# First chunk of a Fourier-mixing and gated-MLP kernel: another order of the weight pieces, and a later place for the combinations of w_out

## The chip, the cores and the metric

The kernel runs on one core of one Trainium2 chip. The metric is the device time of one execution in microseconds (us). The kernel before took 1979.93 us, the median of 8 runs (1978.81 to 1985.56).

## The reference

Two stages in a row. The first takes the real part of a two-dimensional Fourier transform over sequence and model dimension. The second is an MLP with a hard-swish gate.

```python
x: (8, 3008, 256) float32;  w_in: (256, 2048) float64;  w_out: (2048, 256) float64

X = np.fft.fft(np.fft.fft(x, axis=1), axis=2).real.astype(np.float32)
h = X.reshape(24064, 256) @ w_in
g = h * np.clip(h + 3.0, 0.0, 6.0) / 6.0
out = (g @ w_out).astype(np.float32)
```

[...] 

## The kernel before, in words

**Transform.** The eight sequences are taken as four pairs. The sequence transform is done in two stages on TensorE (`stage1`, `stage2`) with a trip through DRAM (`zd`, loaded back by `load_g`) between them. The result of a group of rows is `q`, with `qn` for one extra column. The transform over the model dimension is not done on the data: it is multiplied into w_in (`fold_w_in`, with the matrix `C`), which gives `W1`, and `WN` for the extra column.

**Weights.** w_in and w_out are cut into 16 pieces of 128 x 512 numbers, listed in `PIECES` (L498). Eight are of w_in (two halves `i` of four column blocks `n`), eight of w_out (two halves of four blocks). A piece goes through these steps:

- `load_w` (L506): a DMA issued by GpSimd brings the words into a tile `st`.
- `exponent_a` (L528, ScalarE, two instructions at L532): the exponent bits into a tile `PM`, twice.
- `mantissa` (L547, VectorE, L553 and L554): the mantissa, into `top`.
- `exponent_b` (L534): the two parts of the exponent are subtracted, either on TensorE by two matmuls into a PSUM bank (L542) or on VectorE into an SBUF tile (L538).
- `exponent_c` (L544, ScalarE): makes a power of two of it.
- `join` (L557, VectorE): mantissa times power of two. For w_in it writes a tile `wi` (L562), for w_out two blocks of `G` (L568).

`head(j)` is exponent_a, mantissa and the issue of a later load; `tail(j)` is exponent_c and join; `unit(j)` is exponent_b of piece j, head of piece j+1, tail of piece j.

`fold_w_in(n, h)` multiplies half `h` of column block `n` of w_in with `C`: 8 matmuls into a PSUM tile (L591). Its copy into `W1` (ScalarE, L602) is put off in a list `copies`. While the kernel is starting, a second set of matmuls of one column each (`pw`, L598) makes the `WN` column; later the column is spread by DMAs of SyncE out of `W1` (L607).

**Steps.** A chunk is 256 rows of `q` and its MLP takes 8 steps, `fc` = 0 to 7. A step is `mlp1` (first product into two PSUM tiles `u` and `v`, L337; then VectorE s, u, v, a, a with two ScalarE relus, L342 to L382) and a second product. Step fc needs the columns fc and fc+8 of `W1`, so it needs column blocks of two blocks of w_in: blocks 0 and 2 of w_in serve steps 0 to 3, blocks 1 and 3 serve steps 4 to 7. In the first chunk the second product is `mlp2_first` (L400): four plain block products with the blocks of w_out as they are. From the second chunk on it is `mlp2` (L414): seven products with a Strassen-like scheme. That one needs combinations of the activations (`combine`, GpSimd, three instructions at L396) and of the weights (`mix_w_out`, GpSimd, four instructions at L577 to L580). `mix_w_out(j)` overwrites one of the plain blocks of steps 2j and 2j+1, so it must follow these steps of the first chunk.

**Order.** The order on each engine is the order in which the program text issues the instructions; no scheduler moves them. During the first chunk the main loop (L794 on) issues, in step s: `mlp1` of step s+1, the pending folds, the pieces `DUE[s][0]`, `mlp2_first` of step s, two DMAs that finish the store of `zd`, and the pieces `DUE[s][1]`; then `mix_w_out(0)` to `mix_w_out(2)` in steps 4 to 6. Later steps issue `mlp1` of step s+2, `combine` of step s+1, and `mlp2` of step s; `mix_w_out(3)` stands in step 9. Outside of the start, an exponent on TensorE takes the PSUM tag `d`, which has one bank, and `u`, `v` take a tag `uv`, which has three.

Of the kernel before, what the change touches and what calls it, by code (L numbers as in the profile page):

```python
# [7 lines left out]
F32 = mybir.dt.float32  # L8
# [50 lines left out]
def kernel(  # L59
# [10 lines left out]
    nc = tc.nc  # L70
    P = nc.NUM_PARTITIONS
# [3 lines left out]
    NF = NFC // 2  # L75
# [118 lines left out]
    def bank(shape, name):  # L194
        if starting[0]:
            return ps_a.tile(shape, F32, tag="acc", name=name)
        return ps_d.tile(shape, F32, tag="d", name=name)
# [129 lines left out]
    def mlp1(ch, fc):  # L327
        gr, of, nq = ch.ck // 2, ch.ck % 2 * TB, ch.nq
        q, qn = ch.pr.q[gr], ch.pr.qn[gr]
        u = ps_h.tile([P, 2, TB], F32, tag="uv", name="u")  # L330
        v = ps_h.tile([P, 2, TB], F32, tag="uv", name="v")
        for blk, ps in ((0, u), (1, v)):

            r = slice(0, P - blk)
            for i in range(2):
                f = fc + i * NF
                nc.tensor.matmul(ps[:, i, 0:nq], W1[r, blk, f * P:(f + 1) * P], q[r, blk, of:of + nq],  # L337
                                 start=True, stop=True)
        s = spool.tile([P, 2, TB], F32, tag="s", name="s")
        for i in range(2):  # L340
            f = fc + i * NF
            nc.vector.scalar_tensor_tensor(s[:, i, 0:nq], qn[:, of:of + nq], WN[:, f:f + 1], u[:, i, 0:nq],  # L342
                                           op0=AL.mult, op1=AL.add)


        a = apool.tile([P, 2, 2, TB], F32, tag="a", name="a")
        t = spool.tile([P, 2, 2, TB], F32, tag="t", name="t")
        ch.a[fc] = a
        if ch.last:
            activate_last(a, t, s, u, v, nq)  # L350
            return
        nc.vector.tensor_tensor(u[:], s[:], v[:], op=AL.add)  # L352
        relu(t[:, 0], u[:], 1.0 / 6.0)
        nc.vector.tensor_tensor(v[:], v[:], s[:], op=AL.subtract)  # L354
        relu(t[:, 1], v[:], -1.0 / 6.0)
        gate(a[:, 0], t[:, 0], u[:])
        rev, tk, vk = (m.rearrange("p i (k n) -> p (i k) n", n=N2) for m in (a[:, 1], t[:, 1], v[:]))
        gate(rev[:, :, ::-1], tk, vk)
# [25 lines left out]
    def combine(ch, fc):  # L384
        a = ch.a[fc][:].rearrange("p m f n -> p (m f) n")[:, :, 0:ch.n]
        c = cpool.tile([P, 4, TB], F32, tag="c", name="c")
        cn = c[:, :, 0:ch.n]

        eng = nc.vector if ch.final and fc == NF - 1 else nc.gpsimd
        add(cn[:, 0:2], a[:, 2:3].to_broadcast([P, 2, ch.n]), a[:, 3::-3], eng)  # L390
        add(cn[:, 2], cn[:, 0], a[:, 0], eng)
        add(cn[:, 3], a[:, 1], cn[:, 2], eng)
        ch.c[fc] = cn
# [6 lines left out]
    def mlp2_first(ch, fc):  # L400
        a = ch.a.pop(fc)
        for h in range(2):
            if fc == 0:
                ch.acc[h] = ps_a.tile([P, 2, TB], F32, tag="acc", name="acc")
            for f in range(2):
                nc.tensor.matmul(ch.acc[h][:], G[:, (B11, B12, B21, B22)[2 * f + h], fc, :], a[:, :, f],  # L406
                                 start=(fc == 0 and f == 0), stop=(fc == NF - 1 and f == 1))
        if fc == NF - 1:
            ch.r = epool.tile([P, 2, 2, TB], F32, tag="r", name="r")
            for h in range(2):  # L410
                for m in range(2):
                    nc.scalar.mul(ch.r[:, m, h], ch.acc[h][:, m], (1 - 2 * m) / WS)
# [82 lines left out]

    NWI, NWO = FF // 512, NF // 2
    WB = 512
    PIECES = [("in", 0), ("in", NWI // 2), ("out", 0), ("in", 1), ("in", NWI // 2 + 1)]  # L498
    PIECES = [(k, n, i) for k, n in PIECES + [("out", j) for j in range(1, NWO)] for i in range(2)]
    assert NWI == 4 and NWO == 4  # L500
    raw, difs, exs, fracs, w = {}, {}, {}, {}, {}

# [30 lines left out]

    def exponent_b(j):  # L534
        pm = [PM[j % 2][:, i].bitcast(F16) for i in range(2)]
        if j >= 4 and j % 2:
            exs[j] = wpool.tile([P, WB], F32, tag="ex", bufs=2, name="ex")
            nc.vector.tensor_tensor(exs[j][:], pm[0], pm[1], op=AL.subtract)  # L538
            return
        exs[j] = ps_h.tile([P, WB], F32, tag="uv", name="ex") if starting[0] else bank([P, WB], "ex")  # L540
        for i in range(2):
            nc.tensor.matmul(exs[j][:], E[:, i], pm[i], start=(i == 0), stop=(i == 1))  # L542
# [40 lines left out]
    def fold_w_in(n, h):  # L583

        nb = WB // 2
        cs = slice(n * WB + h * nb, n * WB + (h + 1) * nb)

        ps = bank([P, 2, nb], "wps") if starting[0] else spare[len(copies) % 2]
        for blk in range(2):
            for i in range(2):  # L590
                nc.tensor.matmul(ps[:, blk], C[:, i, blk * P:(blk + 1) * P],  # L591
                                 w["in", n, i][:, h * nb:(h + 1) * nb], start=(i == 0), stop=(i == 1))
        fs = range(cs.start // P, cs.stop // P)

        pw = bank([P, nb // P], "pw") if starting[0] else None
        for f in fs if starting[0] else ():
            for i in range(2):
                nc.tensor.matmul(pw[:, f - fs[0]:f - fs[0] + 1], w["in", n, i][:, (f % (WB // P)) * P:(f % (WB // P) + 1) * P],  # L598
                                 C[:, i, D - 1:D], start=(i == 0), stop=(i == 1))

        def copy():
            nc.scalar.copy(W1[:, :, cs], ps[:])  # L602
            if pw is not None:
                nc.scalar.copy(WN[:, fs[0]:fs[-1] + 1], pw[:])
                return
            for f in fs:
                nc.sync.dma_start(out=WN[:, f:f + 1], in_=W1[P - 1:P, 1, f * P:(f + 1) * P])  # L607

        copies.append(copy)
# [32 lines left out]
        t = T[r, b].rearrange("p g a k n -> p g (a k n)")  # L642
        nc.scalar.copy(t, Z[r].unsqueeze(1).to_broadcast([N2, NG, 2 * TB]))

    folds, copies = [], []

    def head(j):
        exponent_a(j)  # L650
        mantissa(j)
        if j in NEXT:
            load_w(NEXT[j])

    def tail(j):
        exponent_c(j)
        join(j)
        if j % 2 and PIECES[j][0] == "in":
            folds.extend((PIECES[j][1], h) for h in range(2))

    def unit(j):
        exponent_b(j)
        if j + 1 < len(PIECES):
            head(j + 1)
        tail(j)

    def fold_all():
        while folds:
            fold_w_in(*folds.pop(0))
            if len(copies) == 2:  # L670
                copy_all()

    def copy_all():
        while copies:
            copies.pop(0)()

# [19 lines left out]
    load_g(first, 0)  # L698

    seen = wpool.tile([P, 1], F32, tag="seen", name="seen")  # L700
    nc.gpsimd.tensor_copy(seen[:], first.g[0][:, 0, 0:1])
    for j in range(4, 8):
        load_w(j)

# [7 lines left out]
    head(2)  # L712
    tail(1)
    exponent_b(2)
    fold_w_in(*folds.pop(0))
    head(3)
    tail(2)
    exponent_b(3)
# [2 lines left out]
    for i in range(2):  # L721
        stage2(first, 0, i)
    spread(first, 0)
    fold_w_in(*folds.pop(1))
    copy_all()
    starting[0] = False
    spare = [ps_a.tile([P, 2, WB // 2], F32, tag="acc", name="spare") for h in range(2)]
# [52 lines left out]
    def chunk(s):  # L780
        p, ck, fc = steps[s]
        return chunks[p][ck], fc


    DUE = [((), (6,)), ((7,), (8, 9)), ((10, 11), (12,)), ((13,), (14,)), ((15,), ())] + [((), ())] * 3
    head(4)
    mlp1(*chunk(0))
    exponent_b(4)
    head(5)
    tail(4)  # L790
    fold_all()
    unit(5)
    prev = None
    for s, (p, ck, fc) in enumerate(steps):  # L794
        if ck == 0 and fc == 0:
            at = beside(p)
        for f, a in at.get(ck * NF + fc, ()):
            f(*a)
        if s < NF:

            mlp1(*chunk(s + 1))
            fold_all()
            for j in DUE[s][0]:
                unit(j)
            if s == NF - 1:
                combine(*chunk(NF))
            mlp2_first(*chunk(s))
            for dst, src in later[2 * s:2 * s + 2]:
                nc.sync.dma_start(out=dst, in_=src)
            for j in DUE[s][1]:  # L810
                unit(j)
            if 4 <= s < NF - 1:
                mix_w_out(s - 4)
            if s == NF - 1:
                mlp1(*chunk(NF + 1))
        else:
            if s + AHEAD < len(steps):
                mlp1(*chunk(s + AHEAD))
            if s + 1 < len(steps):
                combine(*chunk(s + 1))  # L820
            if s == NF + 1:
                mix_w_out(NWO - 1)
            if prev and fc < 3:
                if fc > 0:
                    store(prev, fc - 1)
                elif not prev.first:
                    finish(prev)
            mlp2(*chunk(s))
        if fc == NF - 1:
            prev = chunks[p][ck]  # L830
# [81 lines left out]
```

## Time and profile before

| | |
|---|---|
| median of 8 runs | 1979.93 us |
| the profiled execution, its own time | 1979.88 us |
| its span, first to last instruction | 1978.0 us |
| TensorE busy in the span | 1943.8 us (98%) |
| VectorE / ScalarE / GpSimd busy | 1442.0 / 687.0 / 1399.8 us |
| TensorE busy, 50 to 100 us from the start | 38.87 of 50 us, granted clock 0.90 |
| TensorE busy, 150 to 175 us from the start | 25.00 of 25 us, granted clock 1.00 |

A busy time is the sum of the instructions of an engine; matmuls are pipelined, and each lasts a little longer than the distance to the next. The granted clock is the share of TensorE's full clock that the chip let it have. Times in the trace are counted from the first instruction. An idle time carries the name of what ended it. The step's first MLP product of the first chunk begins at 49.81 us; the first seven-product step begins at 131.63 us.

### The profile page before, as it was taken

What the parts mean: (1) busy time and instruction counts of PE and PEld (TensorE: products, weight loads), DVE (VectorE), ACT (ScalarE), POOL (GpSimd) and SP (SyncE); (2) the same over time, 40 slices, a digit from 0 to 9 for tenths busy, and PEclk for the clock granted to TensorE, in tenths of its full rate; (3) what the DMA queues carried; (4) which work ended last, traced back from release to release, by engine and by line L of the source; (5) the groups of instructions that cost most, each with busy time, mean ns of one, the idle gap of its engine ahead of it and who ended that gap; (6) DMA issues with size and microseconds to landing.
All of it is one profiled execution on the core that took longest, in us unless ns stands there. A gap on an engine that the chain in (4) does not pass through costs nothing.

```text
span 1978.0 us, 27573 instructions
## 1 busy us (share of the span) xinstructions
PE 1943.8 (98%) x9110; PEld 1670.9 (84%) x9110; DVE 1442.0 (73%) x2780; ACT 687.0 (35%) x1165; POOL 1399.8 (71%) x1592
## 2 busy tenths in 40 slices
PE   9799999999999999999999999999999999999998
PEld 4568888888998888888898888888889888888887
DVE  6786767667787776776777776777678777777776
ACT  5533333333333333333333333333333333333332
POOL 3157778776687787777768877778667667666765
PEclk9899999999999999999999999999999999999999
DMA  8512121121112111220111221212110101111000
GB/s 231 182 39 55 51 56 47 48 56 35 27 36 51 41 49 48 54 60 24 36 32 30 63 55 44 56 41 54 37 22 23 30 14 25 26 23 28 17 21 20
DMA packets 145277, 93.34 MB, mean 47 GB/s; under 512 B 117319, under 2 KB 130635, under 8 KB 145134
## 3 DMA queue, kind: packets, MB, share of 16 engines
q1 hardware_dynamic: 134870, 57.89, 12.2%
q0 software_dynamic: 9472, 33.49, 5.9%
q8 instruction: 72, 1.18, 0.2%
q14 instruction: 71, 0.58, 0.1%
q10 hardware_dynamic: 792, 0.20, 0.0%
HBM read 54.22 MB, written 37.32 MB: 46 GB/s over the span
## 4 chain that ended last, share of the span: by engine, by line
PE 92%; DVE 4%; ACT 2%; DMA 1%; issue 1%; SPq 0%; POOL 0%; DVEq 0%; ACTq 0%; POOLq 0%
PE acc L422 55%; PE v L337 16%; PE u L337 16%; PE ps L213 2%; PE ps L286 2%; DMA xt<-in_x_dram,IX 1%; DVE a L382 1%; DVE s L342 1%; PE acc L406 1%; ACT t L379 1%; ACT PM L532 0%; DVE o L480 0%; PE spare L591 0%; DVE u L352 0%; DVE u L363 0%
## 5 line engine op out<-in xcount | busy, mean ns | idle before, releaser
L396 POOL TENSOR_TENSOR c<-a 128x512 f32<-128x512 f32 (+1 forms) x375 | 468.2, 1248 | 408.1 <-PE acc L422 362.5
L422 PE MATMUL acc<-c,G 128*128 128x256 f32 (+1 forms) x3008 | 696.9, 374 | 0.0
L379 ACT ACTIVATE t<-u,half 128x512 f32<-128x512 f32 (+1 forms) x384 | 260.6, 679 | 1104.9 <-DVE u L352 1025.6
L422 PEld LDWEIGHTS acc<-c,G 128*128 128x128 f32 x3008 | 565.4, 190 | 71.1
L342 DVE SCALAR_TENSOR_TENSOR s<-qn,WN,u 128x256 f32<-128x256 f32 (+1 forms) x768 | 330.3, 471 | 351.9 <-PE u L337 351.4
L422 PE MATMUL acc<-a,G 128*128 128x256 f32 (+1 forms) x2256 | 538.8, 374 | 0.0
L422 PEld LDWEIGHTS acc<-a,G 128*128 128x128 f32 x2256 | 423.4, 190 | 54.9
L337 PE MATMUL v<-q,W 127*128 127x256 f32 (+1 forms) x1536 | 389.1, 375 | 4.2 <-DVE a L382 4.2
L337 PE MATMUL u<-q,W 128*128 128x256 f32 (+1 forms) x1536 | 387.9, 375 | 0.0
L382 DVE SCALAR_TENSOR_TENSOR a<-t,u 128x512 f32<-128x512 f32 (+2 forms) x448 | 263.8, 601 | 102.4 <-ACT t L379 97.3
L337 PEld LDWEIGHTS u<-q,W 128*128 128x128 f32 x1536 | 285.9, 190 | 57.6 <-issue 16.6
L337 PEld LDWEIGHTS v<-q,W 127*128 127x128 f32 x1536 | 288.0, 189 | 44.7 <-DVE a L382 4.6
L396 POOL TENSOR_TENSOR c<-a,c 128x256 f32<-128x256 f32 (+1 forms) x375 | 268.5, 716 | 29.4
L396 POOL TENSOR_TENSOR c<-c,a 128x256 f32<-128x256 f32 (+1 forms) x375 | 268.2, 715 | 29.4
L352 DVE TENSOR_TENSOR u<-s,v 128x512 f32<-128x512 f32 x352 | 245.0, 696 | 38.1 <-DVE s L342 1.8
L382 DVE SCALAR_TENSOR_TENSOR a<-t,v 128x512 f32<-128x512 f32 (+1 forms) x480 | 263.4, 565 | 0.5
L379 ACT ACTIVATE t<-v,half 128x512 f32<-128x512 f32 (+1 forms) x384 | 260.5, 678 | 1.0 <-PE acc L422 0.8
L354 DVE TENSOR_TENSOR v<-v,s 128x512 f32<-128x512 f32 x352 | 243.8, 693 | 0.0
L396 POOL TENSOR_TENSOR r<-w,e 128x256 f32<-128x256 f32 (+1 forms) x92 | 88.7, 986 | 3.6
L430 ACT ACTIVATE e<-acc 128x512 f32<-128x512 f32 (+2 forms) x186 | 84.4, 544 | 3.4 <-PE acc L422 3.3
L480 DVE STREAM_TRANSPOSE o<-r 128x256 f32<-128x256 f32 (+1 forms) x192 | 72.5, 415 | 0.3
L213 PE MATMUL ps<-y,F 94*96 94x512 f32 x120 | 61.3, 601 | 5.2 <-ACT q L289 5.2
(96 smaller groups left out, 798.3 us busy)
## 6 DMA issues: line engine op xcount, KB each, us to landing
out_dram<-o SPq DMA_DIRECT2D x746, 32.0 KB
zd<-z SPq DMA_DIRECT2D x24, 384.0 KB
g<-zd SPq DMA_DIRECT2D x36, 256.0 KB
xt<-in_x_dram POOLq DMA_DIRECT2D x21, 384.0 KB, 4.3
qn<-qd SPq DMA_DIRECT2D x19, 256.0 KB
st<-in_moe_w_in_dram POOLq DMA_DIRECT2D x8, 512.0 KB, 8.3
st<-in_moe_w_out_dram POOLq DMA_DIRECT2D x8, 512.0 KB, 4.0
g<-zd SPq DMA_DIRECT2D x12, 257.0 KB
```

The source lines that it names most:

```text
L213: nc.tensor.matmul(ps[0:PZ], F[0:PR, 0:PZ], y[:, 2 * i:2 * i + 2, :], start=True, stop=True)
L286: nc.tensor.matmul(ps[:, blk, u * P:n].rearrange("p (b k) -> p b k", b=2), g[:, kk, blk * (P + 1):blk * (P + 1) + P], T[:, :, gr, blk, kk, ...
L337: nc.tensor.matmul(ps[:, i, 0:nq], W1[r, blk, f * P:(f + 1) * P], q[r, blk, of:of + nq], start=True, stop=True)
L342: nc.vector.scalar_tensor_tensor(s[:, i, 0:nq], qn[:, of:of + nq], WN[:, f:f + 1], u[:, i, 0:nq], op0=AL.mult, op1=AL.add)
L352: nc.vector.tensor_tensor(u[:], s[:], v[:], op=AL.add)
L354: nc.vector.tensor_tensor(v[:], v[:], s[:], op=AL.subtract)
L379: nc.scalar.activation(t, h, AF.Relu, bias=half[:], scale=scale)
L382: nc.vector.scalar_tensor_tensor(dst, t, 1.0, h, op0=AL.min, op1=AL.mult)
L396: (eng or nc.gpsimd).tensor_tensor(out, in0, in1, op=AL.add)
L422: nc.tensor.matmul(ch.acc[i // 2][:, i % 2, 0:ch.n], G[:, i, fc, :], mv, start=(fc == 0 and i % 2 == 0), stop=(fc == NF - 1), skip_group_c ...
L430: nc.scalar.mul(ch.e[:, k:i + 1, 0:ch.n], ch.acc[i // 2][:, 0:i + 1 - k, 0:ch.n], 1.0 / WS)
L480: nc.vector.transpose(o[:, 0:n // DH, h], ch.r[:, m, h, 0:n].rearrange("p (j i) -> p j i", i=DH))
```

## The change

1. In `PIECES` the second block of w_out moves ahead of the second half of w_in. Before: in 0, in 2, out 0, in 1, in 3, out 1, out 2, out 3. After: in 0, in 2, out 0, out 1, in 1, in 3, out 2, out 3 (two pieces each).
2. `exponent_b`: only the pieces 5 and 15 are subtracted on VectorE; before, 5, 7, 9, 11, 13 and 15. The others go through TensorE and the one bank `d`.
3. The folds are called by name (`fold_now`). Those of blocks 1 and 3 stand in step 3, which has an order of its own (`fourth_step`): `mlp2_first` of step 3 first, then pieces 10 to 13 and the first-half folds between them, then `mlp1` of step 4, then the second-half folds. Every fold with h = 0 makes its `WN` columns by `pw` matmuls, in a `uv` tile; only those with h = 1 use DMAs.
4. In all other steps of the first chunk the second product comes directly after `mlp1`, and the pieces after it. `DUE` follows.
5. `mix_w_out(0)` and `(1)` are issued in step 5, after a one-column copy on GpSimd (`see`) that reads the activations of step 6; `(2)` and `(3)` in steps 8 and 9.

```diff
-    PIECES = [("in", 0), ("in", NWI // 2), ("out", 0), ("in", 1), ("in", NWI // 2 + 1)]
-    PIECES = [(k, n, i) for k, n in PIECES + [("out", j) for j in range(1, NWO)] for i in range(2)]
+    PIECES = [("in", 0), ("in", NWI // 2), ("out", 0), ("out", 1), ("in", 1), ("in", NWI // 2 + 1)]
+    PIECES = [(k, n, i) for k, n in PIECES + [("out", j) for j in range(2, NWO)] for i in range(2)]
...
-        if j >= 4 and j % 2:
+        if j in (5, len(PIECES) - 1):
...
-        pw = bank([P, nb // P], "pw") if starting[0] else None
-        for f in fs if starting[0] else ():
+        pw = ps_h.tile([P, nb // P], F32, tag="uv", name="pw") if h == 0 else None
+        for f in fs if h == 0 else ():
...
-    DUE = [((), (6,)), ((7,), (8, 9)), ((10, 11), (12,)), ((13,), (14,)), ((15,), ())] + [((), ())] * 3
+    DUE = [(6,), (7,), (8, 9), (), (14,), (15,), (), ()]
     head(4)
     mlp1(*chunk(0))
     exponent_b(4)
     head(5)
     tail(4)
-    fold_all()
+    fold_now(0, 1)
+    fold_now(NWI // 2, 1)
+    copy_all()
     unit(5)
+    def fourth_step():
+        mlp2_first(*chunk(3))
+        fold_now(1, 0)
+        unit(10)
+        copy_all()
+        unit(11)
+        exponent_b(12)
+        fold_now(NWI // 2 + 1, 0)
+        head(13)
+        tail(12)
+        copy_all()
+        exponent_b(13)
+        tail(13)
+        mlp1(*chunk(4))
+        fold_now(1, 1)
+        fold_now(NWI // 2 + 1, 1)
+        head(14)
+        copy_all()
...
-            mlp1(*chunk(s + 1))
-            fold_all()
-            for j in DUE[s][0]:
-                unit(j)
-            if s == NF - 1:
-                combine(*chunk(NF))
-            mlp2_first(*chunk(s))
+            if s == 3:
+                fourth_step()
+            else:
+                mlp1(*chunk(s + 1))
+                if s == NF - 1:
+                    combine(*chunk(NF))
+                mlp2_first(*chunk(s))
             for dst, src in later[2 * s:2 * s + 2]:
                 nc.sync.dma_start(out=dst, in_=src)
-            for j in DUE[s][1]:
+            for j in DUE[s]:
                 unit(j)
-            if 4 <= s < NF - 1:
-                mix_w_out(s - 4)
+            if s == 5:
+                see(chunk(s + 1)[0].a[s + 1][:, 0, 0, 0:1])
+                mix_w_out(0)
+                mix_w_out(1)
...
-            if s == NF + 1:
-                mix_w_out(NWO - 1)
+            if s < NF + 2:
+                mix_w_out(s - NF + 2)
```

`see(x)` is `nc.gpsimd.tensor_copy(seen[:], x)`; `fold_now(n, *hs)` calls `fold_w_in(n, h)` for each h; `fold_all`, which took the folds from a list and copied after every two, is gone.

More of the change, by code (lines that the diff above doesn't have):

```diff
@@ L643 @@
         nc.scalar.copy(t, Z[r].unsqueeze(1).to_broadcast([N2, NG, 2 * TB]))
-    folds, copies = [], []
+    copies = []
     def head(j):
@@ L657, in tail @@
         join(j)
-        if j % 2 and PIECES[j][0] == "in":
-            folds.extend((PIECES[j][1], h) for h in range(2))
     def unit(j):
@@ L665, in unit, with fold_now @@
         tail(j)
[L667 to L671, printed above, removed]
+    def fold_now(n, *hs):
+        for h in hs:
+            fold_w_in(n, h)
     def copy_all():
@@ L675, in copy_all, with see @@
             copies.pop(0)()
+    def see(x):
+        nc.gpsimd.tensor_copy(seen[:], x)
     for c in ORDER[0:3]:
@@ L700 @@
     seen = wpool.tile([P, 1], F32, tag="seen", name="seen")
-    nc.gpsimd.tensor_copy(seen[:], first.g[0][:, 0, 0:1])
+    see(first.g[0][:, 0, 0:1])
     for j in range(4, 8):
@@ L714 @@
     exponent_b(2)
-    fold_w_in(*folds.pop(0))
+    fold_now(0, 0)
     head(3)
@@ L723 @@
     spread(first, 0)
-    fold_w_in(*folds.pop(1))
+    fold_now(NWI // 2, 0)
     copy_all()
```

## The prediction

> **What bounds the kernel now.** I read the page, then TensorE's waits, then the first 140 us by windows and by instruction.
>
> ```profile
> PE 1943.8 (98%) x9110; PEld 1670.9 (84%) x9110; DVE 1442.0 (73%) x2780; ACT 687.0 (35%) x1165; POOL 1399.8 (71%) x1592
> PE spare L591 <- ACT W L602: 5.3, 1, 5.3
> PE ps L213 <- ACT q L289: 5.2, 8, 0.7
> PE acc L406 <- DVE G L568: 4.6, 3, 2.5
> PE v L337 <- DVE a L382: 4.2, 7, 1.5
> ```
>
> TensorE bounds the run. Of its named waits, 24.8 us in all, 14.8 lie between 50 and 131.6 us, the first and third of these lines among them; later steps have nearly none (TensorE 25.00 of 25 us between 150 and 175). So the change is worth what it does there, and everything after should move along unchanged. TensorE in the middle of that:
>
> ```profile
> 73.78 1.03 PE L591 MATMUL spare<-wi,C 128*128 128x256 f32 x4
> 80.10 6.18 PE L591 MATMUL spare<-wi,C 128*128 128x256 f32 x16 [5.29 <-ACT W L602]
> 86.12 0.59 PE L542 MATMUL ex<-PM,E 128*128 128x512 f16 x2
> 89.18 1.13 PE L406 MATMUL acc<-a,G 128*128 128x512 f32 x2 [2.47 <-DVE G L568]
> 91.51 1.69 PE L406 MATMUL acc<-a,G 128*128 128x512 f32 x2 [1.21 <-DVE G L568]
> ```
>
> The second pair of folds waits 5.29 us for ScalarE to copy the first pair, and that copy stands behind the relus of step 3, which wait for VectorE. Then pieces 10 and 11 of w_out are awaited, 2.47 and 1.21. The folds that follow take 6.02 us to the next start; the same 16 matmuls took 3.45 at 52.06. The windows say why (columns: TensorE, weight loads, DVE, ACT, POOL, granted clock):
>
> ```profile
> 74.88:78.29 3.41, 0.00 (x0) 0.00 (x0) 3.31 (x6) 0.07 (x1) 2.15 (x3) 1.00 0.35 119
> 78.29:81.70 3.41, 1.60 (x4) 1.34 (x5) 2.88 (x5) 2.24 (x4) 0.00 (x0) 0.50 0.02 0
> 81.70:85.11 3.41, 3.41 (x10) 2.70 (x9) 0.00 (x0) 0.58 (x1) 0.00 (x0) 0.50 0.06 1
> 85.11:88.53 3.42, 1.60 (x8) 0.89 (x6) 0.00 (x0) 2.21 (x4) 0.00 (x0) 1.00 0.06 1
> 88.53:91.94 3.41, 1.56 (x3) 0.59 (x4) 3.20 (x8) 3.33 (x6) 0.07 (x1) 1.00 0.75 214
> 91.94:95.36 3.42, 3.42 (x5) 1.35 (x4) 1.28 (x2) 0.08 (x1) 0.77 (x1) 0.50 0.86 273
> ```
>
> The clock halves at 78.29, returns at 85.11, halves at 91.94, returns at 95.36: all on a grid of 3.41 us. A window busy for 1.56 us or less is followed by half clock; 1.60 was enough to hold it. Loss: 6.02 - 3.44 = 2.6 and, for six records at 91.51, 4.38 - 2.58 = 1.8; together 4.4 us. Last, GpSimd slows VectorE:
>
> ```profile
> 73.07 1.28 DVE L553 TENSOR_SCALAR top<-st 128x512 int32<-128x512 int32 x1
> 74.13 0.80 POOL L578 TENSOR_TENSOR G<-G 128x256 f32<-128x256 f32 x1
> 80.21 0.42 DVE L553 TENSOR_SCALAR top<-st 128x512 int32<-128x512 int32 x1
> ```
>
> The same mantissa instruction takes 1.28 us beside `mix_w_out` and 0.42 alone. From 73.07 to 76.53 VectorE does what takes 1.66 without it: 1.8 us late, in front of the relus and copies just named.
>
> **The change, part by part.** Durations, as start to next start in the timeline: on TensorE first product 1.73, second product 3.44, one fold 1.73, `pw` 0.79, one exponent 0.43. On VectorE a mantissa 1.06, a join 0.60 (w_in) or 0.67 (w_out), the five instructions of a step 3.68 (59.36 to 63.04). On ScalarE a pair of L532 1.33, one L545 0.58. Hand-overs: exponent on TensorE to L545 0.63 (95.89 to 96.52), from there to the join 0.61.
>
> *Added on TensorE.* Four more exponents (pieces 7, 9, 11, 13): 4 x 0.43 = 1.7. Two `pw`: 1.6. Both lie in TensorE's order, none is hidden: +3.3. In return VectorE loses four L538 (0.60 each) and SyncE four small DMAs; neither is on the path there.
>
> *The new order, walked.* Up to 64.00 (second product of step 1) nothing differs but piece 6, a w_out piece whose join is 0.07 longer. Then:
> - Second product of step 1 to 67.44, exponent 7, first product of step 3 to 69.60. Step 2's activations are ready at 68.6, join 7 writes its first block by 70.2, and that is needed at 70.46: the second product of step 2 ends at 73.04 without a wait. Exponent 8 ends at 73.47.
> - Exponent 9 needs the one bank back, so join 8. ScalarE reaches L545 of piece 8 after the relus of step 3 and piece 9's L532, at 74.75; join 8 ends at 76.05. TensorE waits 2.6.
> - Exponent 9, second product of step 3 (to 79.96), fold and `pw` (82.48), exponent 10 (82.91). The pieces 10 to 12 now form a chain through the bank: 0.63 + 0.61 + 0.69 + 0.04 = 2.0 from one exponent to the next, of which TensorE works 0.43. It waits 1.5 for join 10. The second link is 2.5, since the fold's copies and a pair of L532 hold L545 until 85.6: 2.1 for join 11. Exponent 12 ends at 87.39.
> - Fold and `pw` to 89.91, exponent 13, first product of step 4 to 92.07, two folds to 95.53, first product of step 5 to 97.26. Step 4's activations (VectorE from 91.82) are ready at 95.5, so the second product of step 4 ends at 100.70 without a wait.
> - Steps 5 to 7 have no wait on this walk: exponent 14, first and second products to 111.47, `stage2` 0.89, 114.09, 117.53. VectorE is about 2 us ahead each time.
> - First products of steps 9 and 10; the second one's `v` waits 1.55 for the activations of step 9, as now at 130.66 (1.53). The first seven-product step starts at 122.6.
>
> It starts at 131.63 now: 9.0 us gained before any clock loss. Cross-check: waits counted as above, drain included, sum to 7.8 now planned; in the trace they are 13.9 named from 64.00 on, and nine drains of 0.17 (a first product's half lasts 1.03, its start distance is 0.86), 15.5 in all. So -7.7 of waits, -4.4 of half clock, +3.3 of work = -8.8.
>
> *New half-clock windows.* The 2.6 wait, and the 1.5 + 2.1 pair with 0.43 between, can each leave a grid window under 1.6 busy. Where the grid falls against them I can't know. Bounds: none, 0; two full windows, 2 x 1.7 = 3.4. The nearest row is the second drop, also after two gaps of one to three us: 1.8. I take 1.8. [...]
>
> *The mixes moved.* (0) and (1) start when step 6's activations exist, about 105.8, and last 8 x 0.81 = 6.5, to 112.3; they are needed at 122.6. Beside them VectorE has only piece 15's subtraction and join to be slowed, by up to 0.9 (1.10 to 0.69 for L554 at 103.12); the join is due at 108.9 and would end its first block at 108.7: 0. The instructions of a step are not slowed (0.69 beside L578 at 113.96). (2) is new in step 8: 3.1 us, by (3) now (137.81 to 140.92). Queued behind it are combines 10 to 12 and a fold of x. Their first results stand at 136.3, 142.2 and 147.3 now, and TensorE asks at 142.4, 148.1 and 152.8; GpSimd is idle 0.8 ahead of combine 10, so they come 2.3 later, and 3.2 or more stays. Cost 0; bounds 0 and 3.1.
>
> *SyncE.* The four column DMAs of steps 6 and 7 go at 96.6, after the copies; behind them in the queue two `zd` stores, two T loads, and the load of group 1, issued 3.75 after the stores as now (92.40 to 96.15): 104. It took 6 us to clear (96.15 to 102.1), so 110, and `stage2` asks at 111.5. Now it has 18 us to spare, then 1.5. I count 0; up to 2 if it is late.
>
> **Sum.** -9.0 + 1.8 = -7.2. The profiled execution took 1979.88 with 1978.0 in the span; the 1.9 around it stays. 1979.9 - 7.2 = **1972.7**. It stands 0.05 from the median, which I neglect.
>
> **The rivals.**
> - *The bank chain is slower than walked.* For: exponent 10 now stands 86.12 to 89.45, 3.3 from start to end of join, because an L532 pair got ahead in ScalarE's queue; after the change ScalarE has such a pair between all of them. Against: on the walk these pairs fit into the wait. At most four links (9 to 12) at 3.3 in place of 2.0: +5.2, 1977.9. No measurable change.
> - *Half clock holds through step 3.* Place: 76.5 to 97.3, TensorE work there 3.44 + 4 x 1.73 + 2 x 0.79 + 4 x 0.43 + 2 x 1.73 = 17.1; at half clock 17.1 more, less 3.6 of waits that it fills: +13.5 on the walk, 1979.9 - 9.0 + 13.5 = 1984.4, slower. It decides from 9.0 lost, over five windows. For: gaps recur over 14 us. Against: slowed work fills the windows, and one full window brought the clock back (85.11).
> - *GpSimd becomes the bound* in steps 9 to 12: 3.1 of mixing unabsorbed, 1975.8. Against: it stood idle 1.21 at 148.89, 1.18 and 1.87 after.
>
> **How the numbers follow.** A measurement of this kernel tells about 0.2%, 4.0 us, from no change: faster is below 1976.0, slower above 1983.9. Forecast as walked, with 0 to 2 half-clock windows, 0.73, its own range 1970 to 1975.5; GpSimd 0.08, mostly still faster; bank chain 0.13; half clock 0.06. Faster 0.78, no change 0.15, slower 0.07. The range takes the walk's best case and reaches to the bank chain: 1969.0 to 1978.5.
>
> **What would show it.** Right: no wait of `spare` for W; waits of exponents 9, 11, 12 for joins, 2.6, 1.5 and 2.1; the first seven-product step at 122 to 125; mantissas all at 0.42 between 70 and 100; at most two half-clock windows between 73 and 95. Wrong: TensorE waiting for L396 after 122, `stage2` waiting for `g`, links of 3 us, or a first seven-product step past 128.

## The result, and the profile after

The changed kernel took 1976.22 us, the median of 13 runs (1973.19 to 1980.6). The kernel before, run beside it, took 1980.52 us over 35 runs. The ratio is 0.9979, 95% interval 0.9972 to 0.9986: 4.2 us faster, 0.21%, just past the 0.2% that the prediction set as the least that can be told from no change; the interval does not contain 1. The forecast was 1972.7; its range held the time, its gain of 7.2 us was too large. The profiled execution took 1974.02 us with a span of 1972.2.

The page's line of engine totals, and TensorE's waits over the whole run (waiter, what ended it, total, times, longest):

```profile
PE 1944.4 (99%) x9134; PEld 1672.9 (85%) x9134; DVE 1437.7 (73%) x2776; ACT 686.6 (35%) x1167; POOL 1398.7 (71%) x1593
PE ex L542 <- DVE wi L562: 5.6, 3, 2.4
PE ps L213 <- ACT q L289: 5.2, 8, 0.7
PE v L337 <- DVE a L382: 2.3, 5, 1.5
...
PE acc L406 <- DVE G L568: 0.9, 1, 0.9
```

The wait of the folds for ScalarE (5.3 before) is gone, and of the 4.6 us for w_out blocks 0.9 is left. In their place stands one new line, the largest of all: exponents that wait for the join of the piece before, which reads the one PSUM bank that they need, three times, 5.6 us. TensorE there, in order of time:

```profile
73.05 0.59 PE L542 MATMUL ex<-PM,E 128*128 128x512 f16 x2
76.08 0.59 PE L542 MATMUL ex<-PM,E 128*128 128x512 f16 x2 [2.44 <-DVE wi L562]
76.51 3.60 PE L406 MATMUL acc<-a,G 128*128 128x512 f32 x8
79.94 1.89 PE L591 MATMUL spare<-wi,C 128*128 128x256 f32 x8
81.67 0.95 PE L599 MATMUL pw<-C,wi 128*128 128x1 f32 x8
82.48 0.59 PE L542 MATMUL ex<-PM,E 128*128 128x512 f16 x2
84.46 0.59 PE L542 MATMUL ex<-PM,E 128*128 128x512 f16 x2 [1.39 <-DVE wi L562]
86.87 1.01 PE L542 MATMUL ex<-PM,E 128*128 128x512 f16 x2 [1.81 <-DVE wi L562]
87.68 3.62 PE L591 MATMUL spare<-wi,C 128*128 128x256 f32 x8
92.66 1.02 PE L337 MATMUL u<-q,W 128*128 128x256 f32 x4
```

Up to 84.46 the walk holds to a few hundredths (76.09, 82.48 and 84.45 were forecast). Then the same eight fold matmuls that took 1.89 at 79.94 take 3.62 at 87.68, and the first product of step 4 starts at 92.66 instead of 90.34. The windows on the 3.41 us grid (TensorE, weight loads, DVE, ACT, POOL, granted clock):

```profile
81.53:84.94 3.41, 2.02 (x14) 1.31 (x13) 1.18 (x3) 1.83 (x5) 0.00 (x0) 1.00 0.00 0
84.94:88.35 3.41, 1.59 (x5) 1.02 (x4) 2.25 (x4) 2.90 (x5) 0.00 (x0) 0.50 0.00 0
88.35:91.77 3.42, 3.42 (x11) 2.76 (x11) 0.75 (x2) 0.59 (x2) 0.00 (x0) 0.50 0.00 0
```

A window with a granted clock of 0.50 is called a half-clock window from here on. There are two, one after the other: the first was busy for 1.59 us and another followed it; after the second, which was full, the clock was back.

**Where the time went.** The start of a run drifts by a few us between profiled executions (the first product began between 48.98 and 52.61; in the three that began after 51.5 a half-clock window lies near 30 us), and everything after the first seven-product step takes 1846.4 to 1846.9 in every kernel here. So the profiles are best compared by the first chunk, from the first product to the first seven-product step. It is that of one profiled execution; the median is that of 5 to 13 runs (35 of the kernel before), and each ratio is to runs of the kernel before taken beside it, with medians of 1980.16 to 1980.98:

| kernel | first chunk, us | half-clock windows in it | median of its runs, us | ratio to before, 95% |
|---|---|---|---|---|
| before | 81.82 | 3 | 1980.52 | 1 |
| after | 75.61 | 2 | 1976.22 | 0.9979 (0.9972 to 0.9986) |
| after, run again (`c_after`) | 76.90 | 3 | 1975.68 | 0.9978 (0.9969 to 0.9987) |
| `hold3`: after, waits filled | 73.25 | 0 | 1971.89 | 0.9959 (0.9945 to 0.9973) |
| `odd_dve`: after without part 2 | 72.11 | 1 | 1971.48 | 0.9953 (0.9939 to 0.9967) |
| `mix_early`: after without part 5 | 75.00 | 2 | 1977.57 | 0.9984 (0.9975 to 0.9993) |
| `col_dma`: after without `pw` | 74.34 | 2 | 1973.91 | 0.9968 (0.9956 to 0.9980) |
| `before_hold`: before, waits filled | 77.73 | 0 | 1976.11 | 0.9978 (0.9969 to 0.9987) |
| `before_latemix`: before with part 5 | 77.88 | 2 | 1977.19 | 0.9981 (0.9972 to 0.9990) |
| `odd_hold` | 70.71 | 0 | 1970.26 | 0.9948 (0.9935 to 0.9962) |
| `best1` | 69.45 | 0 | 1969.56 | 0.9948 (0.9934 to 0.9962) |
| `best2` | 69.10 | 0 | 1967.48 | 0.9935 (0.9921 to 0.9949) |

### The profile page after: what moved, and what is told of

Its sections match the earlier page's. It is cut to its first block, busy times and chain, and to the rows that moved or that the text cites. A ratio compares the mean times of both kernels' runs of the same rounds, so it can differ in the third digit from the quotient of the medians.

```text
span 1972.2 us, 27615 instructions
## 1 busy us (share of the span) xinstructions
PE 1944.4 (99%) x9134; PEld 1672.9 (85%) x9134; DVE 1437.7 (73%) x2776; ACT 686.6 (35%) x1167; POOL 1398.7 (71%) x1593
## 4 chain that ended last, share of the span: by engine, by line
PE 93%; DVE 3%; ACT 1%; DMA 1%; issue 1%; SPq 0%; DVEq 0%; POOL 0%; ACTq 0%; POOLq 0%
PE acc L422 55%; PE v L337 16%; PE u L337 16%; PE ps L213 2%; PE ps L286 2%; DMA xt<-in_x_dram,IX 1%; DVE a L382 1%; PE acc L406 1%; DVE s L342 1%; ACT t L379 1%; PE spare L591 0%; DVE o L480 0%; DVE u L363 0%; ACT PM L532 0%; DMA T<-in_c_stage_dram 0%
```

## The experiments

**The changed kernel again.** No edit.

> The changed kernel again, for another fall of the 3.41 us clock grid and a tighter ratio. Theory (the walk is right, and the half-clock windows after the waits for the one exponent bank are what was mis-sized): ratio to before 0.998, single runs spread over 1973 to 1981 as the grid falls, and the profile has one to three half-clock windows between 73 and 95 us, with the first seven-product step at 122.6 plus about 1.2 us for each. Rival (the loss against the walk lies elsewhere, in the slowed join of piece 15 or later than 125 us): the same ratio, but a start of the first seven-product step that doesn't go with the number of half-clock windows.

Median 1975.68 over 11 runs (1973.32 to 1980.75). Its profile caught another fall of the grid:

```profile
72.22:75.63 3.41, 1.31 (x5) 0.34 (x4) 3.19 (x6) 3.41 (x6) 0.00 (x0) 1.00 0.60 192
75.63:79.04 3.41, 3.06 (x5) 1.45 (x5) 2.69 (x6) 2.81 (x5) 0.71 (x1) 0.50 0.51 151
...
85.87:89.28 3.41, 2.02 (x5) 0.89 (x5) 2.69 (x5) 2.94 (x5) 0.00 (x0) 0.50 0.00 0
89.28:92.70 3.42, 3.42 (x11) 2.66 (x9) 0.75 (x2) 0.58 (x1) 0.00 (x0) 0.50 0.00 0
```

Here the wait ahead of exponent 9 fell well into a window too. Three windows at half clock, and the first seven-product step at 126.62: four us past the walk's 122.6, where two windows gave 125.44. The start goes with the number of windows, at about 1.2 us each: none, two and three give first chunks of 73.25 (`hold3`, next), 75.61 and 76.90.

**Waits filled with idle matmuls.** The five matmuls of a constant add nothing to the output.

```diff
+    def hold(n):
+        for i in range(n):
+            nc.tensor.matmul(spare[1][:].rearrange("p a b -> p (a b)"), ones[:], C[:].rearrange("p a b -> p (a b)"), start=True, stop=True)
...
             for j in DUE[s]:
+                if j == 9:
+                    hold(2)
                 unit(j)
...
         copy_all()
+        hold(1)
         unit(11)
+        hold(2)
         exponent_b(12)
```

> Adds five idle-time matmuls of the constant C into an unused PSUM tile: two ahead of exponent 9, one ahead of exponent 11, two ahead of exponent 12; 0.86 us each, inside waits of 2.44, 1.39 and 1.81 us. Their results are not used. Theory: no half-clock window is left between 73 and 95 us, so the first seven-product step starts at 122.6 to 123.2 instead of 125.4, the runs spread less, and the ratio to before is 0.995 to 0.997 (1971 to 1974 us). Rival (half clock there is covered by the chain of exponent, ScalarE and join, and costs nothing): 0.998 as without them, or above.

Median 1971.89, ratio 0.9959, five runs within 2.1 us of each other. TensorE in `hold3`:

```profile
82.74 0.59 PE L542 MATMUL ex<-PM,E 128*128 128x512 f16 x2
83.17 1.02 PE L800 MATMUL spare<-C,ones 128*128 128x512 f32 x2
84.72 0.59 PE L542 MATMUL ex<-PM,E 128*128 128x512 f16 x2 [0.53 <-DVE wi L562]
85.15 1.88 PE L800 MATMUL spare<-C,ones 128*128 128x512 f32 x4
87.10 0.59 PE L542 MATMUL ex<-PM,E 128*128 128x512 f16 x2
87.53 1.89 PE L591 MATMUL spare<-wi,C 128*128 128x256 f32 x8
```

The exponents stand where they stood (this execution began 0.2 us later), the work between them is useless, and the fold behind takes 1.89 instead of 3.62. No window is at half clock. The first chunk is 73.25 us; the walk, which had no clock loss, gave 122.6 - 49.8 = 72.8. So 2.4 us of the profiled execution (75.61) and 3.7 of the second one (76.90) were half clock, and by the medians about 4. The granted clock of the single runs agrees: 0.995 to 0.997 in those of the changed kernel, the slowest of them (1980.6) at 0.995 and the fastest (1973.19) at 0.997, and 0.998 to 0.999 in the five of `hold3`.

**Odd pieces back on VectorE.**

```diff
-        if j in (5, len(PIECES) - 1):
+        if j >= 4 and j % 2:
```

> Undoes part 2 of the change alone: pieces 5, 7, 9, 11, 13 and 15 subtract their exponents on VectorE, as before. Theory (the single exponent bank sets the pace of step 3): the wait ahead of exponent 9 is gone, exponents 9 and 11 no longer stand between TensorE and its products, the first product of step 4 starts about 2 us earlier at full clock, and the time falls by 1 to 3 us against the changed kernel (ratio to before 0.9965 to 0.9975). Rival (VectorE is what sets step 3, so that four more instructions of 0.6 us on it cost): 1 to 3 us slower than the changed kernel, 0.9985 to 0.9995.

Median 1971.48, 4.2 us below the 1975.68 of the changed kernel and better than expected. TensorE's waits in `odd_dve`:

```profile
PE ex L542 <- ACT PM L532: 3.1, 5, 1.9
...
PE acc L406 <- DVE G L568: 1.5, 2, 0.9
PE acc L406 <- DVE a L382: 0.7, 1, 0.7
```

No exponent waits for a join any more; the longest wait left is exponent 12, 1.9 us for ScalarE. With every window at full clock (`odd_hold`, below) the first chunk is 70.71 against 73.25: part 2 of the change, which puts these exponents through the one bank, costs 2.5 us; the rest of the 4.2 goes with half-clock windows, one here against two and three. VectorE had most of the room, as it sat idle 4.65 us ahead of join 10 in the changed kernel. Not all: TensorE now waits for it twice where it did not, 0.57 us for the join of piece 7 and 0.75 for the activations of step 3, and the 2.5 are what is left after that.

**Combinations at their old place in the new order.**

```diff
-            if s == 5:
-                see(chunk(s + 1)[0].a[s + 1][:, 0, 0, 0:1])
-                mix_w_out(0)
-                mix_w_out(1)
+            if 4 <= s < NF - 1:
+                mix_w_out(s - 4)
...
-            if s < NF + 2:
-                mix_w_out(s - NF + 2)
+            if s == NF + 1:
+                mix_w_out(NWO - 1)
```

> Undoes part 5 alone: combinations of w_out 0, 1 and 2 issued in steps 4, 5 and 6 and 3 in step 9, without the one-column copy ahead of them. Theory (in the new order of pieces VectorE waits in step 3 anyway, so slowing it there costs nothing): GpSimd runs combination 0 at about 77 us beside a mantissa and a join, combination 1 at about 80 to 83 us in VectorE's idle time, 2 at about 109 us beside piece 15; the ratio stays at 0.998, within 0.5 us. Rival (the later place of the combinations is what the change gained): 2 to 3 us lost, ratio 0.999 to 1.000.

Ratio 0.9984 (0.9975 to 0.9993) against 0.9978 (0.9969 to 0.9987) for the unchanged one: 1.9 us by the medians, with intervals that overlap, and a first chunk of 75.00 us with as many half-clock windows as the 75.61 of the change. The medians speak for the late place and the two first chunks, 0.6 us apart, against it; this run does not settle what it is worth in the new order.

**Combinations late, alone, on the kernel before.** The same edit the other way round on the old order.

```diff
-            if 4 <= s < NF - 1:
-                mix_w_out(s - 4)
+            if s == 5:
+                nc.gpsimd.tensor_copy(seen[:], chunk(s + 1)[0].a[s + 1][:, 0, 0, 0:1])
+                mix_w_out(0)
+                mix_w_out(1)
...
-            if s == NF + 1:
-                mix_w_out(NWO - 1)
+            if s < NF + 2:
+                mix_w_out(s - NF + 2)
```

> Part 5 of the change alone, on the kernel before: combinations 0 and 1 in step 5 after the one-column copy, 2 and 3 in steps 8 and 9, pieces and folds as they were. Theory (in the old order VectorE stood in front of the copies of the folds, so slowing it counted): the mantissas near 73 us take 0.42 us, the wait of 5.29 us falls to about 3.5, 2 to 3 us gained, ratio 0.9985 to 0.999. Rival (the part matters as little in the old order as in the new): 0.9995 to 1.0005.

Ratio 0.9981 (0.9972 to 0.9990), more than expected: this part alone gains 3.8 us by the medians (2.0 to 5.5 by the interval), where the whole change gains 4.2. In this kernel:

```profile
75.45 0.42 DVE L553 TENSOR_SCALAR top<-st 128x512 int32<-128x512 int32 x1
80.70 5.41 PE L591 MATMUL spare<-wi,C 128*128 128x256 f32 x16 [3.50 <-ACT W L602]
```

The mantissa that took 1.28 us beside a combination takes 0.42, and the wait of the folds falls from 5.29 to 3.50, the 1.8 us that the walk had for it. One half-clock window fewer and the wait for step 5's activations, 1.49 us at 110.11 in the kernel before and gone here, make the rest of the 3.9 us by which the first chunk is shorter. By the medians the parts of the change do not add: parts 1 to 4 without part 5 (`mix_early`) gain 3.0, part 5 alone 3.8, both together 4.2. That the late combinations shorten a wait which the new order does not have at all would account for it; the intervals are too wide to show it.

**The half clock of the kernel before.** Seven idle matmuls of a constant, five between the two pairs of folds, two ahead of the second product of step 2.

```diff
             if len(copies) == 2:
                 copy_all()
+                if folds:
+                    keep_awake(5, by=C[:].rearrange("p a b -> p (a b)"))
...
+            if s == 2:
+                keep_awake(2, by=C[:].rearrange("p a b -> p (a b)"))
             mlp2_first(*chunk(s))
```

> The kernel before with seven idle-time matmuls of C (results unused): five between the two pairs of folds where TensorE waits 5.29 us, two ahead of the second product of step 2. It measures the term of 4.4 us for half clock in the kernel before. Theory: no half-clock window between 74 and 100 us, first seven-product step 3 to 4.5 us earlier than 131.6, ratio 0.9975 to 0.9985. Rival (ScalarE and VectorE set the pace there and the slow matmuls were covered): 0.9995 to 1.0005.

Ratio 0.9978, 1976.11 us: filling the waits of the old order gains as much as the whole change. The first chunk is 77.73 against 81.82, so half clock cost the kernel before 4.1 us (4.4 were read off its profile).

**Columns by DMA instead of `pw` in step 3.**

```diff
-        pw = ps_h.tile([P, nb // P], F32, tag="uv", name="pw") if h == 0 else None
-        for f in fs if h == 0 else ():
+        pw = ps_h.tile([P, nb // P], F32, tag="uv", name="pw") if starting[0] else None
+        for f in fs if starting[0] else ():
```

> The changed kernel without the one-column matmuls in step 3: all four later folds spread their columns by DMAs, as before. It measures the term of 1.6 us of added TensorE work. Theory (the matmuls lie on the path and the DMAs would have landed in time): 0.8 to 2 us gained against the changed kernel, ratio 0.9968 to 0.9975; and since these matmuls count as busy in the profile but a window with them still fell to half clock, the number of half-clock windows does not rise without them. Rival (step 4 then waits for its columns): 1 to 3 us lost, VectorE idle ahead of s of step 4, ratio 0.9985 to 0.9995.

Median 1973.91, ratio 0.9968 against 0.9978; first chunk 74.34 against 75.61, both with two half-clock windows. The added matmuls cost 1.3 us of the 1.6 that were counted (1.3 again between `odd_hold` and `best1`, below, where no clock is lost). VectorE does not wait for the columns in step 4: s of that step starts at 93.54, with no idle time ahead of it.

**What was found, put together.** `odd_hold` is `odd_dve` with `hold(2)` ahead of exponent 12. `best1` adds the edit of `col_dma`. `best2` also lets the copy on GpSimd read piece 15's last block:

```diff
-                see(chunk(s + 1)[0].a[s + 1][:, 0, 0, 0:1])
+                see(G[:, B22, NF - 1, 0:1])
```

> The changed kernel with odd pieces subtracted on VectorE and two idle-time matmuls of the constant C (results unused) ahead of exponent 12, where that version waits 1.89 us. Theory (two separate losses: the bank chain, about 2 us, and the half-clock windows, about 2 to 4 us): no half-clock window is left, the first seven-product step starts near 121.5 us when the start of the first product is as in the changed kernel, ratio to before 0.994 to 0.9955. Rival (both versions remove the same loss, the half clock): no gain over either alone, 0.9955 to 0.996.

> Three findings together on the changed kernel: odd pieces subtracted on VectorE, two idle-time matmuls of C ahead of exponent 12 (results unused), and the columns of the later folds by DMA instead of one-column matmuls. Theory (the three losses add up: bank chain, half clock, added matmuls): from the start of the first product to the first seven-product step 69.1 us, against 70.7 without the DMAs and 75.6 to 76.9 in the changed kernel; no half-clock window; ratio to before 0.9935 to 0.9945. Rival (with the rest gone, step 4 waits for its columns): 70.7 us or more, 0.9948 or above.

> best1 with the one-column copy that holds back combinations 0 and 1 reading the last block that piece 15 writes, instead of the activations of step 6. Theory (the join of piece 15, slowed beside combination 0, keeps TensorE 0.36 us in step 6): that join takes 0.75 instead of 1.84 us, 0.3 to 0.4 us gained on the first chunk, within the noise of the time; the combinations end about 4 us later, just before the first combine. Rival (the later combinations hold back the first combines): TensorE waits for GpSimd after the first seven-product step, 0.5 us or more lost.

All three lost every half-clock window in the first chunk: 70.71, 69.45 and 69.10 us. For `odd_hold` 0.9948 is inside what was expected, so bank chain and half clock are two losses. For `best1` the first chunk came out near the 69.1 of the theory, but its time only matched `odd_hold`: 1.3 us of chunk are inside the spread of five runs (1966.62 to 1971.58). `best2` has the lowest ratio, 0.9935 (0.9921 to 0.9949), 12.7 us faster than before by the medians; its own edit is worth 0.35 us in the profile. The join of piece 15 in the changed kernel, and then in `best2`:

```profile
108.61 1.11 DVE L538 TENSOR_TENSOR ex<-PM 128x512 f32<-128x512 f16 x1
109.25 1.06 POOL L578 TENSOR_TENSOR G<-G 128x256 f32<-128x256 f32 x1
110.42 1.84 DVE L568 TENSOR_TENSOR G<-top,ex 128x256 f32<-128x256 f32 x2 [0.69 <-ACT ex L545]
```

```profile
105.24 0.68 DVE L538 TENSOR_TENSOR ex<-PM 128x512 f32<-128x512 f16 x1
106.62 0.76 DVE L568 TENSOR_TENSOR G<-top,ex 128x256 f32<-128x256 f32 x2 [0.70 <-ACT ex L545]
107.52 0.18 POOL L676 COPY seen<-G 128x1 f32<-128x1 f32 x1 [27.67 <-DVE G L568]
```

## Why the prediction was right and where it was off

- *Where the kernel was bound, and that only the first chunk would move*: right. From the first seven-product step to the end it is 1846.37 us before and 1846.76 after.
- *The walk through the new order*: right. Its waits of 2.6, 1.5 and 2.1 (drain included) stand in the profile as 2.44, 1.39 and 1.81 without drain, at its times, and at full clock (`hold3`) the first chunk is 73.25 against its 72.8. With the clock loss taken out of both kernels (`before_hold` and `hold3`) the change is worth 77.73 - 73.25 = 4.5 us; the prediction had 7.7 of waits less 3.3 of work, 4.4.
- *Added work on TensorE, +3.3*: right in place. The `pw` half of it measured 1.3 for 1.6. What the four exponents cost is more than their 1.7 us of work, since they also wait for the bank: 2.5 us in all, but these waits were in the walk.
- *The mixes, cost 0*: off by 0.36 us. Piece 15's subtraction was slowed as reckoned, the join more (1.84 for 0.75), so TensorE's second product of step 6 took 3.96 instead of 3.60. GpSimd did not become the bound, and SyncE's load of group 1 was in time.
- *New half-clock windows, +1.8*: the step that failed, by size. The mechanism was named, with the two gaps that caused it, and its bounds were "none, 0; two full windows, 2 x 1.7 = 3.4". The profiles have two and three windows, 2.4 and 3.7 us, and by the medians (1975.7 to 1976.2 against 1971.89) it is about 4 in a typical run: more windows than were counted, past the upper bound, though each costs less than 1.7. The row I took, the second drop of the kernel before, was a single window followed at once by full work. The first drop in the same table would have told more. It lasts two windows, from 78.29 to 85.11, and lost 2.6: the first of them was busy for 1.60 us at half clock, and half clock followed. So "1.60 was enough to hold it" was read from a window at full clock alone. In the new order work comes in pieces of 0.43 us between waits, the first window at half clock still contained a wait and was busy for 1.59 us (84.94 to 88.35), and half clock followed there too.
- *The sum*: -9.0 + 0.4 + 4.0 = -4.6, against 4.2 to 4.3 measured. The gain at full clock is right; the change has traded 4.1 us of half clock for about as much of its own. That the time lies in the range says little of this term, since the range is 9.5 us wide; and 1976.22 is 0.2 us above the 1976.0 below which the prediction called it faster, a bound set from 1979.9, where the kernel before took 1980.52 beside the change.
- *The rivals*: the bank chain did not run slower than walked. Half clock did not last through step 3. Parts 1, 3 and 4 of the change, the new order itself, were not run apart from each other.

## What to carry to other kernels

When an order is written by hand, walk it at full clock, and then ask of each new wait whether it can cost clock as well: here short pieces of work between waits were followed by 2.4 to 3.7 us of half clock, on top of 5.6 us of waits. A wait that cannot be removed can be filled with idle matmuls; here five of them gained 3.8 us, about as much as the whole reordering had. Parts of a change that remove the same wait are tried one by one, since one alone may give nearly all of it (here, by the medians, the later combinations) while another takes some back (here the exponents on the one bank).

## What the runs showed of the hardware that was not expected

The prediction read off the kernel before that a window busy for 1.56 us falls to half clock and one busy for 1.60 does not. That was no threshold. In both profiles of the changed kernel a window with 2.02 us busy was followed by half clock (81.53 to 84.94 above, and 82.46 to 85.87 in the second), while in `mix_early` this one was not:

```profile
75.48:78.89 3.41, 1.47 (x5) 0.84 (x5) 3.32 (x6) 3.36 (x7) 1.51 (x3) 1.00 0.19 34
78.89:82.31 3.42, 3.42 (x11) 1.88 (x11) 2.46 (x4) 1.08 (x2) 3.26 (x4) 1.00 0.37 137
```

Both windows of the changed kernel contain `pw`, eight records of matmuls with one column each, that the profile shows as 0.95 us busy. `col_dma` has no `pw` in step 3: its window from 82.35 to 85.76 is shown busy for 1.43 us, and it fell too.

So the busy time does not sort the windows. At full clock, windows busy for 0 and 1.56 us (before, 74.88 and 88.53), 1.25 (`odd_dve`, 82.56), 1.31 and 2.02 (`c_after`, 72.22 and 82.46), 1.43 (`col_dma`), 2.02 (after, 81.53) and 2.10 (`mix_early`, 82.31) were followed by half clock; those busy for 1.47 (`mix_early`, above) and 1.60 (before, 85.11) kept the clock. Of the windows at half clock between the first product and the first seven-product step, the five that were followed by another were busy for 1.59 (after, 84.94) to 2.29 us (`col_dma`, from 85.76 on), and those busy for 2.97 (`odd_dve`, 85.97 to 89.38) or more were followed by full clock. Why a window of 2.02 us was followed by half clock and one of 1.47 was not, no run shows.

VectorE's instructions are not slowed alike beside GpSimd's combinations: the join of piece 15, two instructions, went from 0.76 to 1.84 us and the first instruction of a mantissa from 0.42 to 1.28, while the five instructions of a step kept their times (in the kernel before, s 0.86 at 76.53 beside L580, and u, v, a, a 0.70, 0.69, 0.69 and 0.68 from 113.65 on beside L578 to L580). No run shows why.
